# Attention plus a gated MLP on one core: V and K projections moved from the prologue into the background, with a new background pace and order

## The chip, the core and the metric

The kernel runs on one core of one Trainium2 chip. The metric is the device time of one execution in microseconds (us), as the median over several executions. Before the change it was 1062.92 us (4 runs, 1058.0 to 1063.53). Each profile is of one execution; its span is about 2 us shorter than that execution's time.

In this text TensorE is PE in the profile (PEld is its weight load), VectorE is DVE and ScalarE is ACT. "Clock 1.00" and "clock 0.50" are the TensorE clock that the profile says was granted, as a share of full speed.

On states: a run on one core is called slow here when it took over 1.5% longer than the fastest run of the same kernel. Ratios are computed as the mean time of one kernel's fast runs over the mean time of the other's fast runs in the same rounds, so they are not quite the ratio of the medians that are quoted beside them.

## The reference

One sequence of 2048 tokens, width 512, is normalised. A 32-head attention (head size 16) and a ReLU-gated MLP (inner size 1792) both read the normalised input, and their outputs are added to the input.

```python
x  = A_x                                   # [1, 2048, 512] bf16
xn = layernorm(x)
q, k, v = split(xn @ wqkv)                 # 32 heads of 16
p  = softmax(q @ k.T * 16 ** -0.5)         # 2048 x 2048 for each head
A  = (p @ v) @ wo
B  = (relu(xn @ W_gate) * (xn @ W_up)) @ W_down      # inner size 1792
out = x + A + B
```

## The kernel before

The work has a prologue, a main phase and a tail.

The prologue loads x, computes the layernorm statistics, transposes the normalised input into `xnT`, and then projects. All 16 V tiles, the Q of the first two head groups (4 jobs) and the K of the first two groups (8 jobs) are finished before the main phase starts.

```python
jobs = []
for st in range(NT):                      # 16 V jobs
    jobs.append(("v", st, 0))
for sc in range(4):                       # 4 Q jobs
    jobs.append(("q", 0, sc))
for g in (0, 1):                          # 8 K jobs
    for sc in range(4):
        jobs.append(("k", g, sc))
# ... each job: 4 matmuls [128x128] x [128x512], then one eviction on ScalarE or VectorE
```

The main phase is a loop over 819 score units. A unit computes three or two 512-wide score tiles (alternately), ScalarE takes their exp, and if one is due, TensorE does one PV partial product (16 small matmuls). There are five PV partials in eight units. After that, TensorE gets a slice of background work.

```python
for u in range(NU):                       # 819 units
    # ... PE waits for exp(u-2), whose PSUM set it reuses
    # ... PE: scores of unit u (3 or 2 matmuls);  ACT: exp of unit u
    # ... if a PV partial is due: PE: 16 matmuls; DVE: accumulate
    bg_step(u, BG_BUDGET_NS * (n / 3.0))  # n = 3 or 2, BG_BUDGET_NS = 650.0

def bg_step(now_u, budget_ns, check_age=True):
    spent = 0.0
    started = 0
    while spent < budget_ns:
        # ... take the next job if none is active; at most one start per unit
        # ... PE: the job's next matmul
        spent += job.mm_ns                # 250 for most, 260 for a transpose
```

With 250 ns charged for a matmul, a budget of 650 gives three matmuls in a three-tile unit and two in a two-tile unit: "3,2". The background jobs are, in this order: the Q and K of later groups (written to DRAM through four staging slots and read back), then the MLP, in four blocks of 14 up and 14 gate jobs and four down jobs. Output projection jobs (transposes called `woT`, products called `woM`) appear when a head group ends, and they have priority:

```python
def next_job(now_u, check_age=True):
    for qn in ("jobs_wo", "jobs_glu"):    # output projection first
        q = bg[qn]
        if q:
            job = q[0]
            pres = job_ready(job, now_u, check_age)   # inputs at least LAG = 3 units old
            if pres is not None:
                q.pop(0)
                job.pre_res = pres
                return job
            if qn == "jobs_glu":
                return None
    return None
```

All of this is decided when the program is built: each engine gets a fixed stream of instructions, with semaphores between the streams.

The softmax here doesn't subtract the row's maximum and nothing guards it: scores larger than these inputs give would overflow.

## Time and profile before

| | before |
|---|---|
| time, median | 1062.92 us |
| first exp starts | 54.8 us |
| exps 0 to 371, background work present | 1.244 us each |
| exps 372 to 818, little background work | 1.158 us each |
| last exp ends | 1035.2 us |
| tail after it | 20.8 us |
| time at clock 0.50 within the background phase | 51 us |

The per-exp figures come from the start times of the 819 exps in the trace, counted by unit. The unit at which the background work ends comes from the order of instructions in the built program, and the time at each clock from the clock records of the trace.

The first lines are from the page of before: its span, the engines' busy us and shares, the granted clock in 40 slices (9 is 0.9 or more of full speed, 5 is half), the chain that ended last as shares by engine, and the group of exps (count, then busy us and mean ns, then idle us before them and what ended most of it).

```profile
span 1056.0 us, 25312 instructions
...
PE 928.0 (88%) x11322; PEld 405.4 (38%) x11424; DVE 440.1 (42%) x900; ACT 975.0 (92%) x858; POOL 16.7 (2%) x56
...
PEclk9999999699996899989855555555555555555555
...
ACT 48%; PE 46%; DVE 3%; issue 2%; DMA 1%; DVEq 0%; ACTq 0%
...
L905 ACT ACTIVATE pool<-ps_sc 128x1536 bf16<-128x1536 f32 (+1 forms) x819 | 946.5, 1286 | 35.6 <-PE ps_sc L882 30.6
```

ScalarE is busy for 92% of the span and TensorE for 88%, but neither share says which one limits, because the limits differ by stage. TensorE's share says little about the time here: it is 88% before and after the change, though the time fell by 6%.

The next lines are windows of before, that is busy us of each engine and, in brackets, instructions touching the window, then the clock, the DMA share and GB/s.

```profile
...
core 0: us, PE busy (x) PEld busy (x) DVE busy (x) ACT busy (x) POOL busy (x), PEclk, DMA share, GB/s
210.00:310.00 100.00, 97.69 (x1204) 41.47 (x1221) 46.48 (x87) 96.37 (x83) 0.00 (x0) 1.00 0.15 33
324.10:351.40 27.30, 25.39 (x261) 9.33 (x263) 17.30 (x31) 23.69 (x20) 0.00 (x0) 0.50 0.01 2
600.00:700.00 100.00, 83.95 (x1116) 38.42 (x1116) 28.16 (x67) 99.12 (x88) 0.00 (x0) 0.50 0.02 7
```

In 210:310 us TensorE is 98% busy at full clock and only 83 exps touch the 100 us. In 600:700 us there is hardly any background work, the clock is 0.50, and ScalarE is busy without a break with 88 exps. (A window also counts an instruction that crosses its edge, so the counts are about one high. By start times, undisturbed stretches of the later phase run at 1.13 us per exp, with ScalarE 100% busy, as in 700:800 us; that is ScalarE's floor here.) So before is limited by TensorE while background work lasts, and by ScalarE after that. In 324:351 us the clock was 0.50 while background work was present, and fewer exps passed per microsecond (20 in 27 us).

How the clock got there is visible at the end of an MLP block. These are TensorE lines of the timeline of before; the columns are start us, duration us, engine, line, operation, and the wait in brackets.

```profile
...
180.18 0.38 PE L504 MATMUL ps_bg<-xnT,wgs 128*128 128x512 bf16 x1
180.50 0.39 PE L882 MATMUL ps_sc<-qTb,kTb 32*128 32x512 bf16 x3
180.82 0.56 PE L834 MATMUL ps_pv<-v_aug,pool 128*128 128x17 bf16 x16
181.55 0.39 PE L882 MATMUL ps_sc<-qTb,kTb 32*128 32x512 bf16 x2 [0.16 <-ACT pool L905]
181.92 0.56 PE L834 MATMUL ps_pv<-v_aug,pool 128*128 128x17 bf16 x16
182.76 0.39 PE L882 MATMUL ps_sc<-qTb,kTb 32*128 32x512 bf16 x3 [0.28 <-ACT pool L905]
183.62 0.56 PE L834 MATMUL ps_pv<-v_aug,pool 128*128 128x17 bf16 x16 [0.47 <-DVE acc L847]
184.11 0.60 PE L882 MATMUL ps_sc<-qTb,kTb 32*128 32x512 bf16 x2
184.72 0.59 PE L834 MATMUL ps_pv<-v_aug,pool 128*128 128x17 bf16 x16
185.55 0.63 PE L522 MATMUL ps_bg<-Wd_sb,hT 128*128 128x512 bf16 x1 [0.23 <-issue]
```

From 180.5 us to 185.5 us no background matmul runs (L504 is the last gate job and L522 the first down job), because the down job waits until its inputs are three units old. At 184.1 us the two score matmuls take 0.60 us together where they took 0.39: the clock has fallen, to 0.50 by the clock records. I call such a pause a hole. There are more of them where output-projection jobs take over, with one matmul per unit or four small transposes in two units.

The last lines of before are from its timeline around the start of the main phase.

```profile
...
28.00 15.01 PE L292 MATMUL psP<-wqkv_sb,xnT 128*128 128x512 bf16 x62 [0.22 <-issue]
...
42.85 3.62 PE L309 MATMUL psP<-xnT,Wq_perm 128*128 128x512 bf16 x16
...
46.30 7.07 PE L313 MATMUL psP<-xnT,Wk_pad 128*128 128x512 bf16 x31
...
54.24 0.39 PE L882 MATMUL ps_sc<-qTb,kTb 32*128 32x512 bf16 x3 [0.87 <-DVE kTb L327]
...
54.76 1.45 ACT L905 ACTIVATE pool<-ps_sc 128x1536 bf16<-128x1536 f32 x1 [1.62 <-PE ps_sc L882]
```

V takes 15 us (L292), Q 3.6 us (L309) and K 7 us (L313), and only then does the first exp start (L905).

### The profile page before, as it was taken

How to read it: one execution, taken by the hardware profiler on the slowest of the kernel's cores; microseconds unless marked ns; L12 is line 12 of the kernel's file. 1: busy time of each engine (PE TensorE's matmuls, PEld its weight loads, DVE VectorE, ACT ScalarE, POOL GpSimd, SP SyncE). 2: the span in 40 equal slices, each digit the busy share in tenths (PEclk: the TensorE clock that was granted, in tenths of full speed). 3: DMA queues.
4: the chain of work that ended last, by engine and by line, in shares of the span. 5: the costliest groups of instructions: out<-in, count | busy, mean ns of one | idle time of the engine just before them, and what ended most of it. 6: DMA issues, size and time to landing. Idle time of an engine off the chain costs nothing.

```text
span 1056.0 us, 25312 instructions
## 1 busy us (share of the span) xinstructions
PE 928.0 (88%) x11322; PEld 405.4 (38%) x11424; DVE 440.1 (42%) x900; ACT 975.0 (92%) x858; POOL 16.7 (2%) x56
## 2 busy tenths in 40 slices
PE   2999999999999999999888888888878887887886
PEld 1433344344443344444434333333334333343332
DVE  6345555345446552654324522322225522322226
ACT  6399999899999999999999999999999999999992
POOL 6000000000000000000000000000000000000000
PEclk9999999699996899989855555555555555555555
DMA  6031232103120220220001000000000000000002
GB/s 228 1 101 61 82 71 68 24 23 70 32 71 12 51 68 5 72 51 2 1 2 41 1 1 2 22 1 1 2 1 21 2 2 1 1 1 2 2 1 80
DMA packets 73003, 33.86 MB, mean 32 GB/s; under 512 B 60224, under 2 KB 71232, under 8 KB 72896
## 3 DMA queue, kind: packets, MB, share of 16 engines
q1 hardware_dynamic: 72896, 32.26, 11.1%
q8 instruction: 89, 1.46, 0.6%
q14 instruction: 18, 0.15, 0.0%
HBM read 25.43 MB, written 6.82 MB: 31 GB/s over the span
## 4 chain that ended last, share of the span: by engine, by line
ACT 48%; PE 46%; DVE 3%; issue 2%; DMA 1%; DVEq 0%; ACTq 0%
ACT pool L905 48%; PE ps_sc L882 13%; PE ps_pv L834 11%; PE ps_bg L522 4%; PE ps_bg L504 4%; PE ps_bg L491 4%; PE ps_bg L606 2%; PE ps_bg L553 2%; PE psP L292 1%; PE ps_bg L582 1%; DVE stats L234 1%; PE ps_bg L550 1%; PE psP L313 1%; DVE stg L617 1%; PE psT L264 1%
## 5 line engine op out<-in xcount | busy, mean ns | idle before, releaser
L905 ACT ACTIVATE pool<-ps_sc 128x1536 bf16<-128x1536 f32 (+1 forms) x819 | 946.5, 1286 | 35.6 <-PE ps_sc L882 30.6
L882 PE MATMUL ps_sc<-qTb,kTb 32*128 32x512 bf16 x2048 | 423.0, 511 | 88.5 <-ACT pool L905 81.8
L847 DVE TENSOR_TENSOR acc<-ps_pv,acc 128x272 f32<-128x272 f32 x480 | 212.6, 443 | 468.3 <-PE ps_pv L834 463.1
L834 PEld LDWEIGHTS ps_pv<-v_aug,pool 128*128 128x128 bf16 x8192 | 249.7, 101 | 191.4 <-DVE acc L847 118.4
L834 PE MATMUL ps_pv<-v_aug,pool 128*128 128x17 bf16 x8192 | 297.2, 174 | 5.6 <-DVE acc L847 4.0
L882 PEld LDWEIGHTS ps_sc<-qTb,kTb 32*128 32x128 bf16 x2048 | 82.5, 95 | 342.4 <-ACT pool L905 221.6
L504 PE MATMUL ps_bg<-xnT,wgs 128*128 128x512 bf16 x203 | 64.6, 388 | 1.7 <-issue 0.6
L491 PE MATMUL ps_bg<-xnT,wus 128*128 128x512 bf16 x198 | 62.8, 383 | 2.2 <-issue 0.6
L522 PE MATMUL ps_bg<-Wd_sb,hT 128*128 128x512 bf16 x199 | 61.6, 399 | 2.4 <-issue 1.1
L513 DVE SCALAR_TENSOR_TENSOR hT<-ps_bg,up_sb 128x512 bf16<-128x512 f32 x56 | 38.6, 689 | 22.2 <-PE ps_bg L504 22.1
L498 DVE COPY up_sb<-ps_bg 128x512 f32<-128x512 f32 x56 | 38.6, 689 | 18.2 <-PE ps_bg L491 18.2
L619 DVE TENSOR_TENSOR resb<-ps_bg,resb 128x512 f32<-128x512 f32 x48 | 33.2, 692 | 5.6 <-PE ps_bg L606 5.4
L562 DVE CAST stg<-ps_bg 128x512 bf16<-128x512 f32 x36 | 24.8, 690 | 19.8 <-PE ps_bg L553 11.1
L606 PE MATMUL ps_bg<-Wo_sb,oT_sb 128*128 128x512 bf16 x51 | 30.5, 598 | 2.0 <-DVE stg L617 1.5
L844 DVE COPY acc<-ps_pv 128x272 f32<-128x272 f32 x32 | 14.2, 443 | 33.3 <-PE ps_pv L834 33.3
L553 PE MATMUL ps_bg<-xnT,Wk_pad 128*128 128x512 bf16 x87 | 25.4, 380 | 0.8 <-issue 0.5
L264 PE MATMUL psT<-ident,xn_buf 128*128 128x128 bf16 x64 | 8.6, 302 | 19.2 <-DVE xn_buf L256 17.5
L582 PE MATMUL ps_bg<-ident,o_sb 128*64 128x128 bf16 x128 | 22.0, 290 | 1.5 <-DVE o_sb L857 1.4
L504 PEld LDWEIGHTS ps_bg<-xnT,wgs 128*128 128x128 bf16 x224 | 16.6, 97 | 14.4 <-issue 8.5
L491 PEld LDWEIGHTS ps_bg<-xnT,wus 128*128 128x128 bf16 x224 | 16.6, 96 | 12.6 <-issue 6.9
L522 PEld LDWEIGHTS ps_bg<-Wd_sb,hT 128*128 128x128 bf16 x224 | 15.2, 98 | 15.2 <-issue 10.5
L591 DVE COPY oT_sb<-ps_bg 64x512 bf16<-64x512 bf16 x32 | 13.4, 420 | 10.8 <-PE ps_bg L582 10.4
(44 smaller groups left out, 200.0 us busy)
## 6 DMA issues: line engine op xcount, KB each, us to landing
wgs<-in_B_W_gate_dram SPq DMA_DIRECT2D x56, 128.0 KB, 2.3
wus<-in_B_W_up_dram SPq DMA_DIRECT2D x56, 128.0 KB, 2.8
kT_scr<-stg SPq DMA_DIRECT2D x24, 128.0 KB, 1.8
kTb<-kT_scr SPq DMA_DIRECT2D x6, 512.0 KB, 3.4
x_sb<-in_A_x_dram SPq DMA_DIRECT2D x4, 512.0 KB, 5.7
out_dram<-stg SPq DMA_DIRECT2D x16, 128.0 KB, 1.7
Wd_sb<-in_B_W_down_dram SPq DMA_DIRECT2D x1, 1792.0 KB, 14.9
wqkv_sb<-in_A_wqkv_dram SPq DMA_DIRECT2D x1, 1536.0 KB, 10.5
```

The source lines that it names most:

```text
L491: fns.append(lambda e, pf, ph, dt=dt, slot=slot, sc=sc: e.matmul(pf, wus[:, slot, dt, :], xnT[:, dt, 512 * sc:512 * (sc + 1)], start=(dt = ...
L498: upj.evac = (lambda e, pf, ph, us=us: e.tensor_copy(up_sb[:, us, :], pf))
L504: fns.append(lambda e, pf, ph, dt=dt, slot=slot, sc=sc: e.matmul(pf, wgs[:, slot, dt, :], xnT[:, dt, 512 * sc:512 * (sc + 1)], start=(dt = ...
L513: gj.evac = (lambda e, pf, ph, us=us, ft=ft: e.scalar_tensor_tensor(out=hT[:, ft, :], in0=pf, scalar=0.0, in1=up_sb[:, us, :], op0=ALU.max ...
L522: fns.append(lambda e, pf, ph, ft=ft, st=st: e.matmul(pf, hT[:, ft, 128 * st:128 * (st + 1)], Wd_sb[:, ft, :], start=(ft == 0), stop=(ft = ...
L553: fns.append(lambda e, pf, ph, dt=dt, idx_=idx_, sc=sc: e.matmul(pf, Wk_pad[:, dt, idx_, :], xnT[:, dt, 512 * sc:512 * (sc + 1)], start=(d ...
L606: return [lambda e, pf, ph: e.matmul(pf, oT_sb[:, tb, mq, 128 * t:128 * (t + 1)], Wo_sb[:, gg, :], start=True, stop=True)]
L619: wj.evac = (lambda e, pf, ph, m=m: e.tensor_tensor(resb[:, m, :], pf, resb[:, m, :], ALU.add))
L834: ev = PE.op(lambda e, m=m, sl=sl, off=off, kt=kt, h=h: e.matmul(ps_pv[:, m, 0:VN], pool[:, sl, off:off + 128], v_aug[:, kt, h, 0:VN], sta ...
L847: eva = DV.op(lambda e, a=a: e.tensor_tensor(acc[:, a, :, 0:VN], ps_pv[:, :, 0:VN], acc[:, a, :, 0:VN], ALU.add), C_DVE)
L882: ev = PE.op(lambda e, bank=bank, kb=kb, qb=qb, j=j, kt=kt, c4=c4: e.matmul(ps_sc[:, bank, :], kTb[32 * j:32 * j + 32, kb, 128 * kt:128 * ...
L905: ev_exp[u] = AC.op(lambda e, s0=s0, n=n, fb=fb: e.activation(pool[:, s0:s0 + n, :], ps_sc[:, fb:fb + n, :], ACTF.Exp, scale=0.25), C_ACT)
```

## The change

The intent was to start the exps earlier and to load TensorE more evenly. The prologue keeps only four Q jobs and one K job. The V jobs and the remaining seven K jobs become the first background jobs. The background budget falls from 650 to 400, which is two matmuls in every unit ("2,2"). The rest concerns order and waits: two up jobs of the next MLP block go before the down jobs, output-projection jobs alternate with MLP jobs, a transpose is charged 60 instead of 260, and a staging slot waits for its own last write instead of for all four writes of a target. A second copy of the V weights needs SBUF. The stride of V falls from 24 to 20 for it.

```diff
-VW = 24
+VW = 20
-BG_BUDGET_NS = 650.0
+BG_BUDGET_NS = 400.0
@@ prologue
+        ev_wv = SP.op(lambda e: e.dma_start(Wv_sb[:], A_wqkv[:, 2 * D:3 * D]...), C_DW[2])
-        jobs = []
-        for st in range(NT):
-            jobs.append(("v", st, 0))
-        for sc in range(4):
-            jobs.append(("q", 0, sc))
-        for g in (0, 1):
-            for sc in range(4):
-                jobs.append(("k", g, sc))
+        jobs = [("q", 0, sc) for sc in range(4)] + [("k", 0, 0)]
@@ order of the MLP jobs
+            for sc in range(4):
+                for ft in range(FT):
+                    k = sc * FT + ft
+                    if sc == 0 or ft >= 2:
+                        new.append(up[k])
+                    new.append(gate[k])
+                if sc < 3:
+                    new += [up[(sc + 1) * FT], up[(sc + 1) * FT + 1]]
+                new += [down[(sc, st)] for st in range(4)]
@@ early background jobs (bodies cut)
+            order = ["v0", "v1", "v2", "k0_1", "v3", "v4", "v5", "v6", "k0_2", "v7", "v8", "v9", "k0_3",
+                     "v10", "v11", "v12", "v13", "v14", "v15", "k1_0", "k1_1", "k1_2", "k1_3"]
-        bg["jobs_glu"] = make_qk_jobs() + make_glu_jobs()
+        bg["jobs_glu"] = make_early_jobs() + make_qk_jobs() + make_glu_jobs()
@@ transposes of the output projection
-                tj = BGJob("woT%d_%d" % (g, mq), t_mms(), 260.0, pre=list(norm_evs), ...)
+                tj = BGJob("woT%d_%d" % (g, mq), t_mms(), 60.0, pre=list(norm_evs), ...)
@@ staging slots
                 pc = qk_slot_prev_cnt.get(job.slot)
                 if pc is not None:
-                    pres.append(Ev(pc.sem, 64))
+                    pres.append(pc)
@@ next_job
-            for qn in ("jobs_wo", "jobs_glu"):
+            order = ("jobs_glu", "jobs_wo") if bg.get("last") == "jobs_wo" else ("jobs_wo", "jobs_glu")
+            for qn in order:
...
+                        bg["last"] = qn
-                    if qn == "jobs_glu":
-                        return None
@@ the PV partial waits for its V tile, the scores for their K chunk (cut)
```

## The prediction

> **What bounds it now.** The span (1056 us) has three parts in the timeline: a prologue until the first exp at 54.8 us, 819 exps until 1035 us (1.197 us each), and a 21 us tail. Windows split the middle:
> - 210:310 us, background matmuls, clock 1.00: 83 exps, 1.205 us each. TensorE is 97 to 98% busy and limits: the timeline shows 1.26 us per score unit with a PV and two background matmuls, 1.48 us with three, and ScalarE waiting 0.24 us per eight exps for scores.
> - 700:800 us, no background work, clock 0.50: 90 exps, 1.11 us each, ScalarE 100% busy: its floor.
> - Where background work pauses (181 to 185 us before the down projection, 319 to 324 us of transposes) the clock falls to 0.50, and then seven or eight exps fit in 10 us instead of nine. At 105 us ScalarE loses 1.9 us to an eviction that waits for a staging DMA.
>
> **What the change does.**
> 1. Removes 16 V and 7 K jobs (92 matmuls at about 0.216 us) from the prologue. Transposes end at 28 us; five jobs follow, so the first exp should start near 33.5 us: 21 us gained, all critical.
> 2. Those matmuls become background work, but the budget falls from 5 to 4 background matmuls per pair of units. The instruction order shows an even 2 per unit to unit 506 of 819, against 3,2,3,2 to unit 371.
> 3. Removes the holes: two up jobs of the next block stand before the down jobs, output-projection jobs alternate with GLU jobs, four transposes share a unit.
> 4. Staging slots wait for their own last write, ending stalls like that at 105 us. The V stride and the extra load should not matter.
>
> **Cost.** With two background matmuls a PV unit needs 1.26 us of TensorE, one without PV roughly 0.8; five of eight have a PV: mean 1.09 us, just under ScalarE's 1.11 to 1.13. So the background phase goes from TensorE-bound (1.253 us per unit over units 0 to 371, cold stretches included) to nearly ScalarE-bound; I take 1.145. Estimate: 33.5 + 507 x 1.145 + 312 x 1.14 + 21 = 991 us of span; the median before is 5 us above the profiled run, so **995 us**, range **972 to 1035**. Chances: faster by over 2% 0.94, within 2% 0.05, slower 0.01.
>
> **What would show it.** First exp at 33 to 34 us. Clock 1.00 from there to about 610 us with few dips, then 0.50. 87 to 88 exps per 100 us in the background phase, not 82; TensorE below 97% there. ScalarE's wait for scores well under 30.6 us in total, its share of the span 95% or more; tail still 21 us.
>
> **What would make it wrong.** The clock. [...] 1.00 with dense background work, 0.50 without; yet at 330 to 348 us TensorE was over 90% busy, with one background matmul in most units, and stayed at 0.50. If two per unit, or 5 per three units in the alternating stretches, is too thin, a unit at 0.50 costs about 1.7 us (estimate: scores 0.54, two matmuls at 0.43, PV share 0.3): every 100 such units add 55 us. If TensorE's order delays scores more than I think, the phase stays at 1.2 us per unit and the time is near 1023.

## The result, and the profile after

The changed kernel took 1000.79 us (median of 10 timed runs, 999.21 to 1007.93), against 1062.43 us for before over all runs up to then (16). The ratio of fast runs is 0.9439, 95% interval 0.942 to 0.9458. Three of the changed kernel's runs lie at 1004 to 1008 us, with a mean clock of 0.800 to 0.805 instead of 0.807 to 0.811.

The page of after:

```profile
span 998.4 us, 25287 instructions
...
PE 876.9 (88%) x11292; PEld 383.4 (38%) x11424; DVE 449.9 (45%) x911; ACT 954.2 (96%) x847; POOL 16.6 (2%) x56
...
PEclk9999999999999999999999998555555555555555
...
ACT 72%; PE 23%; DVE 2%; DMA 1%; issue 1%; SPq 0%; ACTq 0%; DVEq 0%
...
L945 ACT ACTIVATE pool<-ps_sc 128x1536 bf16<-128x1536 f32 (+1 forms) x819 | 932.3, 1302 | 10.2 <-PE ps_sc L922 6.8
```

ScalarE's share rises to 96%, its wait for scores falls from 30.6 to 6.8 us, and the chain that ended last is 72% ScalarE where it was 48%. The clock is at full speed up to slice 24 without a dip, changes in slice 25 and is half afterwards; by the clock records it changes at 618 us.

The windows of after:

```profile
...
core 0: us, PE busy (x) PEld busy (x) DVE busy (x) ACT busy (x) POOL busy (x), PEclk, DMA share, GB/s
210.00:310.00 100.00, 94.35 (x1253) 40.95 (x1274) 51.86 (x101) 99.40 (x88) 0.00 (x0) 1.00 0.18 44
500.00:600.00 100.00, 91.89 (x1223) 40.07 (x1241) 56.61 (x109) 99.11 (x88) 0.00 (x0) 1.00 0.17 41
700.00:800.00 100.00, 85.66 (x1073) 37.56 (x1074) 38.59 (x81) 96.92 (x86) 0.00 (x0) 0.50 0.02 7
```

In 210:310 us 88 exps now touch the window instead of 83, and TensorE has 6% idle instead of 2%.

The start of the main phase in the timeline of after:

```profile
...
28.01 4.92 PE L288 MATMUL psP<-xnT,Wq_perm 128*128 128x512 bf16 x15 [0.22 <-issue]
...
32.77 1.03 PE L292 MATMUL psP<-xnT,Wk_pad 128*128 128x512 bf16 x4
...
34.52 0.39 PE L922 MATMUL ps_sc<-qTb,kTb 32*128 32x512 bf16 x3 [0.73 <-ACT kTb L304]
...
34.85 0.60 PE L572 MATMUL ps_bg<-Wv_sb,xnT 128*128 128x512 bf16 x2
...
35.04 3.71 ACT L945 ACTIVATE pool<-ps_sc 128x1536 bf16<-128x1536 f32 x3 [0.62 <-PE ps_sc L922]
```

Q (L288) and K (L292) end at 33.8 us, and the first exp (L945) starts at 35.0 us instead of 54.8. The first V job already runs as background work (L572).

The span splits as the prediction split it:

| | predicted | measured in the profile |
|---|---|---|
| first exp | 33.5 us | 35.0 us |
| 507 units with background work | 1.145 us each, 580.5 us | 1.146 us each, 581.2 us |
| 312 units after that | 1.14 us each, 355.7 us | 1.156 us each, 360.7 us |
| tail | 21 us | 21.5 us |
| span | 991 us | 998.4 us |

### The profile page after: what moved, and what is told of

Its sections match the earlier page's. It is cut to its first block, busy times and chain, and to the rows that moved or that the text cites. A ratio compares the mean times of both kernels' runs of the same rounds, so it can differ in the third digit from the quotient of the medians.

```text
span 998.4 us, 25287 instructions
## 1 busy us (share of the span) xinstructions
PE 876.9 (88%) x11292; PEld 383.4 (38%) x11424; DVE 449.9 (45%) x911; ACT 954.2 (96%) x847; POOL 16.6 (2%) x56
## 4 chain that ended last, share of the span: by engine, by line
ACT 72%; PE 23%; DVE 2%; DMA 1%; issue 1%; SPq 0%; ACTq 0%; DVEq 0%
ACT pool L945 71%; PE ps_pv L873 7%; PE ps_sc L922 7%; PE ps_bg L502 2%; PE ps_bg L484 1%; DVE stats L237 1%; PE ps_bg L471 1%; PE ps_bg L614 1%; PE ps_bg L638 1%; PE ps_bg L548 1%; PE psT L267 1%; PE psP L288 0%; DVE stg L649 0%; DMA wus<-in_B_W_up_dram 0%; PE ps_bg L572 0%
## 5 line engine op out<-in xcount | busy, mean ns | idle before, releaser
L945 ACT ACTIVATE pool<-ps_sc 128x1536 bf16<-128x1536 f32 (+1 forms) x819 | 932.3, 1302 | 10.2 <-PE ps_sc L922 6.8
L922 PE MATMUL ps_sc<-qTb,kTb 32*128 32x512 bf16 x2048 | 386.5, 467 | 81.5 <-ACT pool L945 78.2
L873 PEld LDWEIGHTS ps_pv<-v_aug,pool 128*128 128x128 bf16 x8192 | 245.9, 99 | 165.2 <-DVE acc L886 113.3
L873 PE MATMUL ps_pv<-v_aug,pool 128*128 128x17 bf16 x8192 | 293.5, 173 | 3.1 <-DVE acc L886 1.9
L484 PE MATMUL ps_bg<-xnT,wgs 128*128 128x512 bf16 x188 | 59.0, 380 | 3.1 <-issue 1.0
L638 PE MATMUL ps_bg<-Wo_sb,oT_sb 128*128 128x512 bf16 x55 | 26.9, 491 | 2.6 <-DVE stg L649 2.1
L572 PE MATMUL ps_bg<-Wv_sb,xnT 128*128 128x512 bf16 x56 | 17.4, 380 | 0.7 <-issue 0.3
L614 PE MATMUL ps_bg<-ident,o_sb 128*64 128x128 bf16 x128 | 16.3, 269 | 1.5 <-DVE o_sb L896 1.4
L471 PEld LDWEIGHTS ps_bg<-xnT,wus 128*128 128x128 bf16 x224 | 13.2, 96 | 9.9 <-issue 8.8
L484 PEld LDWEIGHTS ps_bg<-xnT,wgs 128*128 128x128 bf16 x224 | 13.2, 96 | 9.3 <-issue 8.2
```

What stands on the lines that cost most here:

```text
L471: fns.append(lambda e, pf, ph, dt=dt, slot=slot, sc=sc: e.matmul(pf, wus[:, slot, dt, :], xnT[:, dt, 512 * sc:512 * (sc + 1)], start=(dt = ...
L484: fns.append(lambda e, pf, ph, dt=dt, slot=slot, sc=sc: e.matmul(pf, wgs[:, slot, dt, :], xnT[:, dt, 512 * sc:512 * (sc + 1)], start=(dt = ...
L638: return [lambda e, pf, ph: e.matmul(pf, oT_sb[:, tb, mq, 128 * t:128 * (t + 1)], Wo_sb[:, gg, :], start=True, stop=True)]
L873: ev = PE.op(lambda e, m=m, sl=sl, off=off, kt=kt, h=h: e.matmul(ps_pv[:, m, 0:VN], pool[:, sl, off:off + 128], v_aug[:, kt, h, 0:VN], sta ...
L922: ev = PE.op(lambda e, bank=bank, kb=kb, qb=qb, j=j, kt=kt, c4=c4: e.matmul(ps_sc[:, bank, :], kTb[32 * j:32 * j + 32, kb, 128 * kt:128 * ...
L945: ev_exp[u] = AC.op(lambda e, s0=s0, n=n, fb=fb: e.activation(pool[:, s0:s0 + n, :], ps_sc[:, fb:fb + n, :], ACTF.Exp, scale=0.25), C_ACT)
```

## The experiments

The total was right, but it lumps several edits together. I took the change apart by three questions: does the prologue count in full, what is the pace worth alone, and what are the holes worth alone? Twelve kernels ran, and all gave correct outputs.

"Holes mended" means the new MLP order, the alternation and the 60 for a transpose together. "Dips" is time at clock 0.50 before the background work ends, in the profiled run.

### Old pace in the changed kernel

```diff
-BG_BUDGET_NS = 400.0
+BG_BUDGET_NS = 650.0
```

> The changed kernel with the old budget (3,2 background matmuls per pair of units instead of 2,2); prologue, holes and semaphores stay mended. Theory (pace): five matmuls per pair make TensorE the limit again, about 1.206 us per unit (the hole-free stretches of before) for some 380 units at clock 1.00 with no dips: about 1022 us. Rival (clock alone): only the dips at 0.50 had cost time, so without them the background phase stays at 1.146 us per unit and the time at about 1001 us.

Measured: 1035.13 us (4 runs, 1033.94 to 1042.21), ratio to before 0.9762 (0.9718 to 0.9805). There were no dips, and 380 background units took 1.230 us each. One window of this kernel, with the columns of the windows above:

```profile
...
210.00:310.00 100.00, 99.51 (x1231) 42.09 (x1231) 49.21 (x97) 96.03 (x83) 0.00 (x0) 1.00 0.20 49
```

TensorE is 99.5% busy at full clock and 83 exps touch the window, as in before. Pace is a cause of its own: with dips absent in both, 3,2 instead of 2,2 costs 34 us. It came out larger than expected (1022 us). Units 0 to 40 took the 1.206 us each of the forecast, but units 80 to 120 took 1.264 and units 240 to 280 took 1.272; there the instruction order shows transposes and projection matmuls in addition to the 3,2.

### Holes back in the changed kernel

```diff
-            (the new MLP order)
-            return new
+            return jl
-            order = ("jobs_glu", "jobs_wo") if bg.get("last") == "jobs_wo" else ("jobs_wo", "jobs_glu")
-            for qn in order:
+            for qn in ("jobs_wo", "jobs_glu"):
...
-                tj = BGJob(..., t_mms(), 60.0, ...)
+                tj = BGJob(..., t_mms(), 260.0, ...)
```

> The changed kernel with the old job order: down jobs directly after the last gate job, output-projection jobs always first, two transposes per unit. Budget 400 and the short prologue stay. Theory (holes): the clock falls to 0.50 in three to five stretches of 7 us or more between 150 and 600 us, as in before, and the time is 10 to 18 us longer, 1011 to 1019 us. Rival (pace alone): with two matmuls per unit TensorE has slack enough to take the holes, so 1001 to 1004 us, dips or not.

Measured: 1055.13, 1055.97, 1081.83 and 1091.31 us; the last two are slow by the rule. Ratio of the fast two to before 0.9935 (0.9905 to 0.9965). Even the fastest run is 54 us over the change, three times what the theory expected, and far outside the rival's 1001 to 1004 us too. The profiled run (1055.97) has eight dips of 10 to 51 us, 212 us in all; its granted clock in 40 slices shows them:

```profile
...
PEclk9999996997755998679995798675555555555555
```

A unit that starts at clock 1.00 takes 1.154 us and one at 0.50 takes 1.543 us.

### The new pace alone, in before

```diff
-BG_BUDGET_NS = 650.0
+BG_BUDGET_NS = 400.0
```

> The kernel before with only the budget changed to 400. Theory: the background phase lasts 480 units instead of 372, at 1.146 us plus some 0.03 for dips; 54.8 + 480 x 1.176 + 339 x 1.155 + 22 = 1033 us span, ratio about 0.972 to before. Rival (the pace only helps when the holes are mended too, since a thinner background lets the clock fall more): no gain or slower, ratio 0.99 to 1.02, with more time at 0.50 inside the background phase.

Measured: 1076.01 us (4 runs, 1073.07 to 1086.04), ratio 1.0144 (1.0091 to 1.0197). The theory fell and the rival holds: the pace alone makes the kernel slower. Units at clock 1.00 did fall from 1.219 to 1.157 us, as the theory wanted, but the dips grew from 51 to 208 us. The longest is shown by this window (the same columns):

```profile
...
307.10:389.00 81.90, 81.01 (x726) 25.54 (x726) 30.88 (x57) 63.33 (x53) 0.00 (x0) 0.50 0.05 11
```

For 82 us TensorE is 99% busy at half clock and the clock does not come back. The dips of before lasted 7, 10, 27 and 7 us. So in these profiles a hole costs little at the old pace, where the clock was back within 27 us, and much at the new pace, where that took up to 82 us.

### Holes mended alone, in before

The edit puts the new order, the alternation and the 60 into before, at the old budget of 650.

> The kernel before with only the holes mended (GLU order, alternation, four transposes per unit) at the old budget of 3,2. Theory: no dip in the background phase; 33 units at 0.50 become 1.22 us units, 0.29 us each, and TensorE stays the limit: 8 to 12 us faster than before, ratio about 0.990. Rival (the holes are most of the gain outside the prologue): 30 us or more faster, ratio 0.97.

Measured: 1054.81 us (4 runs, 1054.03 to 1056.1), ratio 0.9933 (0.9917 to 0.995), no dips, 344 background units at 1.239 us. The gain of about 8 us is at the lower edge of the 8 to 12 us that the theory expected.

### V and K back in the prologue

```diff
-        jobs = [("q", 0, sc) for sc in range(4)] + [("k", 0, 0)]
+        jobs = [("v", st, 0) for st in range(NT)] + [("q", 0, sc) for sc in range(4)] \
+             + [("k", g, sc) for g in (0, 1) for sc in range(4)]
... (the matmuls and the eviction of a V job in the prologue, cut)
-        bg["jobs_glu"] = make_early_jobs() + make_qk_jobs() + make_glu_jobs()
+        bg["jobs_glu"] = make_qk_jobs() + make_glu_jobs()
```

> The changed kernel with all V jobs and the eight K jobs of the first two groups computed in the prologue again; everything else as changed. Theory (the prologue is on the critical path in full, and 92 background matmuls cost nothing while ScalarE is the limit): first exp at about 54.8 us, time 18 to 20 us longer, about 1020 us. Rival (part of the gain is given back, because the moved matmuls load the background phase): under 14 us longer.

Measured: 1020.8 us (4 runs; three at 1019.74 to 1021.67, one slow at 1038.94), ratio 0.9604 (0.9581 to 0.9628), 20.0 us over the change. The first exp starts at 54.9 us. From the first exp to the end of the last it took 942.3 us, against 941.9 us in the change. The 92 moved matmuls cost nothing measurable, and the prologue counts in full.

### The short prologue alone

The edit is the two of "old pace" and "holes back" together, in the changed kernel.

> The changed kernel with the old budget and all holes back: what is left is the short prologue with its moved V and K jobs, and the slot semaphores. Theory (the prologue is a separate term): 19 to 21 us faster than before, 1042 to 1044 us, as far as the old pace recovers the clock fast (dips of 7 to 30 us as in before). Rival (the moved jobs take back part, as they lengthen a phase that TensorE limits by 35 units at some 0.09 us each, 3 us, or bring new dips): 1046 us or more.

Measured: 1045.93 us (4 runs, 1042.48 to 1048.54), ratio 0.9846 (0.9817 to 0.9876): 16.5 us faster than before, between theory and rival. The first exp starts 19.4 us earlier, but the stretch from first to last exp is 984.5 us instead of 980.4. In this pair of profiles (each among the fastest runs of its kernel) the moved matmuls take back about 4 us at the old pace, as the rival said; the runs of this kernel differ by 6 us among themselves, so the 4 us are not sure.

These runs fill a cube. The medians, all in us, with the time at clock 0.50 in the background phase of the profiled run in brackets:

| | old pace 3,2 | new pace 2,2 |
|---|---|---|
| long prologue, holes | 1062.4 (51) before | 1076.0 (208) |
| long prologue, holes mended | 1054.8 (0) | 1020.8 (0) |
| short prologue, holes | 1045.9 (55) | 1068.9 (212), fast runs 1055.5 |
| short prologue, holes mended | 1035.1 (0) | 1000.8 (0) the change |

The two kernels of the long prologue that were made from before (1076.0 and 1054.8) keep the old staging waits, which the slot experiment below finds to be worth nothing in the change. The rounds ran on three chips, each with before in the same rounds (medians 1062.4 to 1062.6). The profile of before is one of its fastest runs (1058.0 us, mean clock 0.723 against 0.715 to 0.720 in most of its other runs), so its typical run had more than 51 us at 0.50, by an estimate from these mean clocks 6 to 17 us more.

### Only one kind of hole back

The first kernel undoes only the MLP order, the second only the alternation and the 60.

> The changed kernel with only the GLU order undone (down jobs directly after the last gate job): four holes of two units without a background matmul come back at units 178, 284, 372 and 479. In the run with all holes back, three such holes were followed by 10 to 24 us at clock 0.50. Theory (any hole tips the clock): 40 to 70 us at 0.50 in the background phase, 26 to 45 units at 1.54 instead of 1.15 us, 10 to 18 us longer than the change: 1011 to 1019 us. Rival (only the long projection holes of 8 to 24 units tip it): no dip, within 3 us of 1001.

Measured: 1000.83, 1011.1, 1027.32 and 1033.67 us (the last two slow by the rule). The ratio of the fast two to before is 0.947 (0.9412 to 0.9528), whose interval overlaps the change's. The profile fell on the fastest run, with one dip of 3.4 us after the last of the four holes. So in this run one of the four holes of two units was followed by a fall of the clock; neither the theory's 1011 to 1019 us nor the rival's "no dip" covers it. The longer runs have no profile, so that their extra time is dips too was not seen, but their mean clocks fit it: 0.795, 0.777 and 0.768, the lower the longer the run. If the rest was at 1.00, that is some 30, 75 and 95 us more at 0.50 than in the change (an estimate), for 10, 27 and 33 us more time. The profiled run holds a surprise: its clock was 0.949 instead of 1.00 through the whole background phase, but for that dip. A background unit took 1.150 us all the same, 0.003 us more than in the change, so a clock that is 5% lower costs almost nothing at this pace while half a clock costs a third (1.543 us against 1.154 in the profile with all holes back).

> The changed kernel with only the projection holes undone (projection jobs first whenever ready, two transposes per unit); the GLU order stays mended. Theory: the stretches of 8 to 24 units around units 108, 215, 317 and 417 bring back some 150 us at 0.50, about 100 units at 0.39 us more, 35 to 40 us longer: 1036 to 1041 us. With the first run of this pair it should add up to the 54 to 55 us of all holes together. Rival (the two kinds of hole need each other): well under half of that.

Measured: 1030.16, 1117.66, 1124.72 and 1125.13 us. All four lie above every run of the change. The profiled run is one of the slow ones, so the following is about that run only: four dips of 58 to 113 us in the background phase and the beginning of the lasting low clock, 401 us in all. Here are windows inside one dip and just after it (the same columns):

```profile
...
213.60:230.70 17.10, 17.10 (x154) 5.08 (x152) 5.98 (x12) 11.91 (x10) 0.00 (x0) 0.50 0.21 47
...
244.30:260.00 15.70, 15.39 (x200) 6.29 (x199) 8.39 (x15) 15.18 (x14) 0.00 (x0) 1.00 0.23 53
```

TensorE is 100% busy for tens of microseconds at clock 0.50, with two background matmuls in every unit, and only 10 exps touch 17 us. The sum was not confirmed: the only fast run is 29 us over the change, which with the 0 to 10 us of the fast runs above makes 29 to 40 us and not 54, while the other three runs are 117 to 124 us over it, more than both kinds of hole cost together. The profiled slow run spent 401 us at 0.50, against 212 us in the fast profile with all holes back. How long a dip lasts at this pace varies too much from case to case to be added up (10 to 51 us there, 58 to 113 us here).

### A still thinner background

```diff
-BG_BUDGET_NS = 400.0
+BG_BUDGET_NS = 300.0
```

> The changed kernel with the budget at 300: 2,1 background matmuls per pair of units, so the background reaches to unit 676. Theory A (1.5 matmuls per unit keeps the clock, as the alternating stretches with 5 per 3 units did): 1.13 us per unit instead of 1.146 and the quiet-phase projection stalls fall away: 8 to 12 us faster than the change, about 990 us. Theory B (1.5 is too thin): dips at 0.50 inside the background phase and 10 us or more slower than the change.

Measured: 1131.08, 1168.55, 1196.35 and 1197.25 us. All runs are far slower than the change; theory B holds, by much more than its 10 us. The profile is of the fastest run. Units at 1.00 took 1.134 us each, which is ScalarE's floor and what theory A wanted. But at 245 us the clock fell and stayed at 0.50 for 522 us, at 1.52 us per unit. It then came back for 140 us, with the same pace of background work, and fell again at 907 us. The first fence holds windows before and in the dip (the same columns), the second the TensorE timeline just before the fall (start us, duration us, instruction, wait):

```profile
...
238.20:241.60 3.40, 3.40 (x48) 1.41 (x44) 1.82 (x4) 3.40 (x5) 0.00 (x0) 1.00 0.00 0
241.60:245.00 3.40, 2.58 (x29) 1.01 (x29) 0.79 (x2) 3.40 (x5) 0.00 (x0) 0.99 0.34 77
300.00:400.00 100.00, 100.00 (x919) 32.39 (x916) 33.94 (x65) 81.88 (x67) 0.00 (x0) 0.50 0.05 12
```

```profile
...
241.00 0.39 PE L922 MATMUL ps_sc<-qTb,kTb 32*128 32x512 bf16 x2
241.32 0.39 PE L471 MATMUL ps_bg<-xnT,wus 128*128 128x512 bf16 x1
241.91 0.39 PE L922 MATMUL ps_sc<-qTb,kTb 32*128 32x512 bf16 x3 [0.19 <-ACT pool L945]
242.23 0.60 PE L471 MATMUL ps_bg<-xnT,wus 128*128 128x512 bf16 x2
242.82 0.39 PE L922 MATMUL ps_sc<-qTb,kTb 32*128 32x512 bf16 x2
243.14 0.39 PE L484 MATMUL ps_bg<-xnT,wgs 128*128 128x512 bf16 x1
244.16 0.39 PE L922 MATMUL ps_sc<-qTb,kTb 32*128 32x512 bf16 x3 [0.63 <-ACT pool L945]
244.49 0.56 PE L873 MATMUL ps_pv<-v_aug,pool 128*128 128x17 bf16 x16
244.90 1.00 PE L484 MATMUL ps_bg<-xnT,wgs 128*128 128x512 bf16 x2
```

There is no hole here: a background job is active in every unit, and the longest pause of TensorE is 0.63 us. Three units without a PV and with four background matmuls between them (the first three pairs above) came just before the fall, and the second fall, at 907 us, also came shortly after three such units in a row. In the dip TensorE is 100% busy, and still the clock did not return for 522 us.

### Staging slots

```diff
-                    pres.append(pc)
+                    pres.extend(tgt_evs[pc])      # all four writes of the slot's previous target
```

> The changed kernel in which a staging slot waits again for all four writes of the previous target, not for its own last write alone. Theory (a write lands 1.8 us after issue, less than the two units of 1.15 us between jobs, so the extra wait seldom bites): 0 to 3 us longer than the change, 1001 to 1004 us. Rival (it is a cause of its own, 2 us for each of nine targets): 1015 us or more.

Measured: 1000.45 us (4 fast runs, 999.62 to 1001.63), ratio to before 0.9421 (0.9399 to 0.9443). No difference from the change, as the theory said. The slot semaphores are not a cause.

### Two attempts at a better version

The first lets a projection job start only in every second unit once no MLP job is left:

```diff
+                    if check_age and not bg["jobs_glu"] and now_u % 2:
+                        return
```

> The changed kernel, but once no GLU job is left a projection job may start only in every second unit. At clock 0.50 a unit with a PV and a projection matmul does not fit into ScalarE's 1.13 us (units 600 to 640 took 1.246 us each, 720 to 760 1.167). Theory: these stretches fall to 1.13 to 1.15, some 5 to 7 us in all, 994 to 997 us. Rival (TensorE's lead is lost by the PV of the four transposed units, not by the projection rate): within 2 us of 1001.

Measured: 997.65 us (6 runs: four at 996.93 to 997.73, two at 1005.42 and 1007.06), ratio 0.9407 (0.9377 to 0.9436). The profile fell on a run with two dips (7 and 21 us), but its quiet phase is undisturbed: 312 units at 1.1475 us instead of 1.1561, 2.7 us less. Units 600 to 640 went from 1.246 to 1.176 us, but the projection then reaches further, and units 640 to 680 went from 1.128 to 1.169. This is half of what was expected. It is the fastest median of all, 3.1 us below the change, and four of its six runs are below the change's fastest; but the two intervals overlap, so it is a likely gain and not a proven one.

The second adds an interleaved prologue: each of the first three Q jobs stands between transposes (after tiles 5, 9 and 13).

> The previous kernel, and the first three Q jobs of the prologue stand between the transposes (after tiles 5, 9 and 13) instead of after them. Theory (TensorE idles 0.29 us per tile pair there, and the prologue is critical): first exp 1 to 2 us earlier than 35 us, 993 to 996 us. Rival (the transposes are paced by the chain over VectorE and ScalarE, which each Q job and its eviction delay by as much as is saved): no difference.

Measured: 1000.86 us (6 runs, 999.3 to 1013.14), ratio 0.9442 (0.9405 to 0.9479). It lost what the first had won. Two lines of its timeline:

```profile
...
20.77 1.91 PE L268 MATMUL psP<-xnT,Wq_perm 128*128 128x512 bf16 x4
...
36.89 1.45 ACT L953 ACTIVATE pool<-ps_sc 128x1536 bf16<-128x1536 f32 x1 [2.69 <-PE ps_sc L930]
```

The first Q job between the transposes ran at half clock by its duration (1.91 us for four matmuls, against 1.03 us for the four of the K job in the change), the transposes waited behind it and its eviction, and the first exp came at 36.9 us instead of 35.0. The expectation was wrong in sign. The rival's chain argument holds for part of it. A dip of 10 us came on top: it began at 33.1 us, before the first exp, so the K job too took 1.91 us instead of 1.03, which is about half of the 1.9 us lost there.

## Why the prediction was right, and where it was not

**The total.** 995 us was forecast and 1000.8 us measured, inside the range of 972 to 1035. The agreement is a little better than the parts deserve: the parts of the span add up to 7.7 us more than forecast, while the forecast had allowed 4 us between the profiled span and the median, which turned out to be 2.4 us.

**The prologue (step 1)** was right. The first exp was forecast at 33 to 34 us and came at 35.0 us (34.0 to 35.4 us in the profiled kernels with the same prologue). The 1.5 us come from the start of the Q jobs: fifteen recorded matmuls take 4.92 us in the change, where sixteen took 3.62 us in before, because the clock comes up only during them, at 31.1 us by the clock records (it came up at 30.5 us, during the V jobs, in before). The other profiled kernels with this prologue agree: where the clock came up at 28.7 us the first exp started at 34.0 us, and where it came up at 31.8 us, at 35.4 us. Putting the work back cost 20.0 us of 21 forecast.

**The cost per background unit** was right to 0.001 us (1.145 against 1.146). So close a hit is partly luck, since 1.145 was a choice a little above a floor that was itself read too low (see the next paragraph). The mechanism behind it was right too: at the old pace in the same kernel, TensorE is 99.5% busy and a unit takes 1.230 us; at the new pace it has 6% idle and ScalarE sets the time. The forecast of the clock (1.00 until about 610 us) was right as well; it changed at 618 us.

**ScalarE's floor** was read wrong. The forecast took "1.11 us each" from 90 exps in a 100 us window, and a window counts exps that cross its edges. By start times it is 1.13 us. It hardly mattered, as 1.145 was used for the sum.

**The quiet phase** is the mis-sized term. "312 x 1.14" was 1.156 and added 5 us; before already had 1.158 there. At clock 0.50, a unit with scores, a PV and a projection matmul does not fit into 1.13 us (units 600 to 640 took 1.246 us each). The change packs the transposes four to a unit there, which takes 1.167 us per unit in units 720 to 760, where before has 1.151. The experiment that thinned the projection jobs there returned 2.7 us.

**The weight of holes (step 3) against pace (step 2)** is where the explanation, not the number, was incomplete. The forecast costed the pace as if it stood alone and mentioned the clock only as a risk. The cube shows that they can't be separated: at the long prologue, mending the holes alone gains 8 us, the new pace alone loses 14 us, and both together gain 42 us. The pace lowers the unit from 1.22 to 1.15 us only while the clock is up, and with it the falls lasted longer: up to 82 us at the long prologue, against up to 27 us in before. The mended holes are what makes the lower pace usable.

**The risk paragraph** was sound. It estimated 1.7 us for a unit at 0.50 with two matmuls; 1.54 to 1.66 us was measured with holes back. It asked whether 5 matmuls per three units is too thin; in the profiled run of the change it was not (no dip), and 1.5 per unit was.

**Slot semaphores (step 4)** had no effect in the change. The V stride was only tried as a build: with a stride of 24 the changed kernel doesn't fit, its tensor `stg2` lacking 2848 bytes per partition. So its own effect on time stays open.

What stays open too: which property of the matmul stream the clock goes with. Busy time as the profile shows it is not it: in the thinnest kernel TensorE was 100% busy from 300 to 400 us, at clock 0.50. The traces hold a better candidate, the number of full-size background matmuls (128 rows, 512 columns) that start in 3.41 us, a length of which the stretches at 0.50 in before are whole multiples (6.83, 10.24, 27.31 and 6.83 us are 2, 3, 8 and 2 times 3.413). Counted in such steps between the clock changes, over the background phases of the twelve experiments' profiles: at clock 1.00, a step with at most two of them was the last before a fall in 25 cases of 36, and one with three or more in 3 of 1442. At 0.50, none of the 28 returns came after a step with fewer than four; with four or more, a step almost free of PV matmuls (at most one) was followed by a return in 24 cases of 47, and one with more PV matmuls in 4 of 147. So 24 of the 28 returns came after a step almost free of PV matmuls. In before, the five steps before a fall have no full-size background matmul on record, and the four before a return have four or five, with at most 16 PV matmuls. This is a count made afterwards, and no experiment changed this property alone.

Why three runs of the change itself are 4 to 7 us longer was not seen in a profile. Their mean clock of 0.800 to 0.805 is, by an estimate, 10 to 20 us more at 0.50; the profiled run of the first attempt at a better version, which is 9 us longer than that kernel's median, had two such dips (7 and 21 us).

## What to carry to other kernels

Where the clock of TensorE falls in thin stretches of work, as it did here (0.50 for 522 us at 1.5 background matmuls per unit), the pace of filler work and the pauses in it are one design decision: first close every pause, then thin the filler until the other engine is the limit, and stop while there is a margin, because in these profiles a fall of the clock could last the longer the thinner the filler was: 3 to 27 us at five background matmuls per two units (before, and the short prologue alone), 3 to 113 us at four, up to 522 us at three. Try such edits together as well as one by one; here one of them alone is a loss and is most of the gain in company. And take more than one run, since the same program got quite different clocks here from run to run (mean 0.768 to 0.795 with only the MLP order undone, 0.661 to 0.762 with only the projection holes back).
